# Weight scales in four groups, a weight decode with one join, and weight tiles asked for later

## The chip, the cores and the metric

The kernel runs on one core of one Trainium2 chip. The metric is the device time of one execution in microseconds (us). The engines are named as in the profile: PE (TensorE, matrix products; PEld its weight loads), DVE (VectorE), ACT (ScalarE), POOL (GpSimd) and SP (SyncE, which here only issues DMA transfers). Each takes its own instructions in order.

## The reference

Inputs are q, k, v of shape (4, 8, 768, 64): 4 batches, 8 heads, 768 positions, 64 numbers per head. Each position of q and k is assigned to the nearest of its head's 16 centroids, attention is allowed only within a cluster, and the result goes through a two-layer network with a squared ReLU, 512 to 2048 to 512 numbers per token. The two weight matrices arrive as 64-bit floats.

```python
q_assign = argmax(einsum('bhsd,hcd->bhsc', q_n, c_n), axis=-1)     # q_n, c_n: normalised
k_assign = argmax(einsum('bhsd,hcd->bhsc', k_n, c_n), axis=-1)
mask = q_assign[:, :, :, None] == k_assign[:, :, None, :]
scores = where(mask, matmul(q, k^T) / sqrt(64), -1e9)
attn = softmax(scores, axis=-1)
x = matmul(attn, v)                      # 3072 tokens x 512
h = x @ w_in                             # w_in 512 x 2048
out = (s * max(h, 0)**2 + b) @ w_out     # w_out 2048 x 512
```

## The kernel before, in words

**Units.** Attention is cut into 192 units, each one tile of 128 query rows of one head: the outer loop goes over batch b, chunk c (256 rows), head pair hp, row tile t and head h. A chunk (b, c) has 16 units. A unit is a score `sc` on PE (`scores`, L464: the masked products of Q with all 768 keys, in two fp16 halves), the row maximum on DVE (`maxima`, L473), the exponential on ACT (`exps`, L483, tile `p`), the fp16 high half of `p` (`high`, on POOL, DVE or ACT, L121 or L119, tile `ph`), the low half by subtraction on POOL (`low`, L506), a DMA transpose into `PT` (L508), and the product with V on PE (`values`, L525 to L527, for two units at once, tile `px`), which DVE scales into `xs` (L533 to L537). The first eight units keep fp32 and transpose on PE instead (L503, L520). After four units `finish_x` makes a transposed tile `x`.

**MLP.** The 512 to 2048 to 512 network is worked off in 192 steps, 16 (one per slice ft of 128 hidden numbers) for each of the 12 chunks. A step is 12 products into `h` (`mlp_in`, L583), three activations on ACT (`mlp_relu`), a subtraction on POOL (`mlp_gl`, L598) and 6 products into the accumulator `acc` (`mlp_out`, L610). Step m stands beside unit m + 21 (`LAG`). `acc` has one place in PSUM; at the end of a chunk DVE evicts it into `o` (L618), scaled, and with the bias row added.

**Weights.** For each ft there is a tile of w_in (`wi`) and one of w_out (`wo`), 32 tiles in all. `weights` is a generator that treats one tile per call in a pipeline of three stages: `fetch` (a 512 KB DMA into `wst`), then two calls later `rebase` (ACT takes the high word to a float of another exponent, L203) and `narrow` (DVE shifts it left by 3, L207, then ORs in the low word shifted right by 29, L208), then `bound` one call later. `bound` writes absolute values with ACT (L215, L217; for w_out with a sum along the row), and for w_in takes column sums of them on PE (L220) and their maximum on DVE (L221). When all 32 tiles are through, `finish_w_in` and `finish_w_out` make one power-of-two scale for each matrix. Only then can `wsplit` cut a tile into two fp16 halves (ACT L265, DVE L267), from step 17 on. The main loop calls the generator twice per unit from unit 0 on. The halves take places of the tag `w`, of which there are 33: 32 for the tiles and one more.

**Order.** The program is written unit by unit with generators for the preparation of K, Q and V (`prep_k`, `prep_q`, `prep_v`, started at the steps in `START`); a list scheduler with priorities then fixes one order per engine before the run. The first 20 units have a higher priority (`first_of_all`). Weight loads are issued by SP behind the last transpose.

## Time and profile before

| | us |
|---|---|
| median of 3 runs | 953.16 |
| lowest, highest | 952.39, 954.72 |
| the profiled execution, its own time | 953.86 |
| its span, first to last instruction | 952.2 |
| exponential of unit 0 starts at | 36.37 |
| of unit 20 | 153.36 |
| of unit 32 | 212.11 |
| of unit 60 | 335.75 |

| engine | busy us | share of the span |
|---|---|---|
| PE | 828.6 | 87% |
| ACT | 711.0 | 75% |
| DVE | 626.1 | 66% |
| POOL | 573.0 | 60% |

A line of a group reads: line, engine, operation, output <- inputs, sizes, count | busy us in all, mean ns of one | idle us of the engine just before them, and what ended it. A line of stretches gives start:end, its length, and for each engine its busy us and number of instructions, then the mean granted clock of PE (1.00 is full), the busy share of the DMA engines and GB/s.

### The profile page before, as it was taken

Reading aid. Unit: us, or ns where it says so; the run is one execution under the profiler, and the core shown is the slowest. Engines: PE = TensorE matmul, PEld = TensorE weight load, DVE = VectorE, ACT = ScalarE, POOL = GpSimd, SP = SyncE. Lnnn points to the kernel's source line nnn. Section 1 sums busy time; section 2 is a strip of 40 time slices with the busy share of each in tenths; the row PEclk is TensorE's granted clock in tenths of the full one; section 3 lists DMA queues with packets and bytes.
Section 4 is the critical chain, followed back from the end, with each engine's and each line's share of the span. In section 5 each row is a group of like instructions: output and inputs, shape, how many; then the busy total and the mean of one; then the engine's idle time right before and its main releaser. Section 6 shows DMA issues by size and latency. Waiting matters only on the chain. (4 is left out here: it accounts for less than half of the span.)

```text
span 952.2 us, 22467 instructions
## 1 busy us (share of the span) xinstructions
PE 828.6 (87%) x8625; PEld 579.4 (61%) x8625; DVE 626.1 (66%) x1400; ACT 711.0 (75%) x1390; POOL 573.0 (60%) x596
## 2 busy tenths in 40 slices
PE   0668446988999989999899999999999999999997
PEld 0457324555666667766566666766666766767764
DVE  7797988999677657767865757668666466463100
ACT  4477656887688778987787877978787888789443
POOL 3012545677578566866767758667776765676321
PEclk9965556999999999999999999999999999999999
DMA  6888974876887796968689969758877757777100
GB/s 182 227 215 234 235 179 92 197 151 114 174 167 154 170 201 122 186 147 181 139 165 177 184 142 181 149 130 189 156 153 170 145 116 152 138 165 133 33 23 22
DMA packets 450300, 147.36 MB, mean 155 GB/s; under 512 B 417937, under 2 KB 446609, under 8 KB 450193
## 3 DMA queue, kind: packets, MB, share of 16 engines
q1 hardware_dynamic: 450192, 145.93, 72.2%
q8 instruction: 67, 1.10, 0.5%
q14 instruction: 41, 0.33, 0.1%
HBM read 35.69 MB, written 6.29 MB: 44 GB/s over the span
## 5 line engine op out<-in xcount | busy, mean ns | idle before, releaser
L506 POOL TENSOR_TENSOR ph<-p,ph 128x768 f16<-128x768 f32 x184 | 312.2, 1697 | 123.7 <-ACT ph L119 76.2
L583 PE MATMUL h<-x,wis 128*128 128x256 f16 x2304 | 287.6, 274 | 9.6 <-ACT r L590 8.0
L610 PE MATMUL acc<-wos,g 128*128 128x512 f16 x1152 | 292.6, 379 | 3.2 <-POOL g L598 2.8
L583 PEld LDWEIGHTS <-wis 128*128 128x128 f16 x2304 | 222.2, 98 | 59.5 <-issue 11.3
L598 POOL TENSOR_TENSOR g<-r,g 128x256 f16<-128x256 f32 x192 | 136.6, 713 | 101.7 <-ACT r L593 97.1
L473 DVE TENSOR_REDUCE ssm<-sc 128x1 f32<-128x768 f32 x192 | 181.5, 951 | 24.4 <-PE sc L464 23.6
L483 ACT ACTIVATE p<-sc,ssm,qsm 128x768 f32<-128x768 f32 x192 | 187.7, 978 | 3.4 <-DMA PT<-ph 1.0
L610 PEld LDWEIGHTS <-g 128*128 128x128 f16 x1152 | 103.6, 97 | 87.8 <-POOL g L598 5.7
L480 ACT ACTIVATE ssm<-ssm,lift,qsm 128x1 f32<-128x1 f32 x192 | 73.1, 381 | 92.5 <-DVE ssm L473 91.7
L119 ACT ACTIVATE ph<-p 128x768 f16<-128x768 f32 x164 | 136.1, 830 | 5.8 <-DMA PT<-ph 4.3
L590 ACT ACTIVATE r<-h,cf 128x256 f32<-128x256 f32 x192 | 89.1, 464 | 56.9 <-PE h L583 49.6
L525 PE MATMUL px<-vh,PT 128*128 128x65 f16 x1104 | 120.4, 197 | 12.9 <-DVE xs L537 6.8
L464 PE MATMUL sc<-KA,QA 128*128 128x384 f16 x384 | 99.9, 343 | 26.4 <-ACT p L483 23.4
L526 PE MATMUL px<-vl,PT 128*128 128x64 f16 x1104 | 120.3, 194 | 0.0
L527 PE MATMUL px<-vh,PT 128*128 128x65 f16 x1104 | 120.0, 195 | 0.0
L525 PEld LDWEIGHTS <-PT 128*128 128x128 f16 x1104 | 103.6, 98 | 23.1 <-issue 14.4
L526 PEld LDWEIGHTS <-PT 128*128 128x128 f16 x1104 | 103.3, 100 | 13.2 <-issue 5.1
L464 PE MATMUL sc<-KB,QB 128*128 128x384 f16 x384 | 100.1, 345 | 7.0 <-DMA QB<-qb 7.0
L527 PEld LDWEIGHTS <-PT 128*128 128x128 f16 x1104 | 103.5, 98 | 2.7
L592 ACT ACTIVATE g<-r 128x256 f16<-128x256 f32 x192 | 79.3, 413 | 4.0
L593 ACT ACTIVATE r<-r 128x256 f32<-128x256 f32 x192 | 78.8, 411 | 3.3
L464 PEld LDWEIGHTS <-QA 128*128 128x128 f16 x384 | 35.9, 101 | 54.9 <-issue 29.2
(156 smaller groups left out, 1032.3 us busy)
## 6 DMA issues: line engine op xcount, KB each, us to landing
wst<-in_moe_w_in_dram SPq DMA_DIRECT2D x16, 512.0 KB, 4.5
wst<-in_moe_w_out_dram SPq DMA_DIRECT2D x16, 512.0 KB, 4.5
kn<-in_k_dram SPq DMA_DIRECT2D x16, 384.0 KB, 4.1
qn<-in_q_dram SPq DMA_DIRECT2D x24, 256.0 KB, 3.5
vn<-in_v_dram SPq DMA_DIRECT2D x16, 384.0 KB, 4.1
out_dram<-o SPq DMA_DIRECT2D x12, 512.0 KB, 3.8
PT<-ph SPq DMA_TRANSPOSE x184, 3.5
x<-xn SPq DMA_TRANSPOSE x48, 2.5
```

Of the source, the lines that this page charges most:

```text
L119: A.activation(dst, src, AF.Copy)
L464: last_score[0] = nc.tensor.matmul(sc[:, e, :HALF], X[:, col, :], y[:, h * S + e * HALF : h * S + (e + 1) * HALF], start=st, stop=not st)
L473: last_max[0] = V.tensor_reduce(SM[i // 4][:, 0, j : j + 1], U[i]["sc"], axis=AX.XY, op=ALU.max, negate=True)
L483: last_exp[0] = A.activation(p.rearrange("p (a b) -> p a b", a=2), u["sc"], AF.Exp, bias=bi, scale=u["scale"], **total)
L506: G.tensor_tensor(u["ph"][:, 1, :], u["p"], u["ph"][:, 0, :], op=ALU.subtract)
L525: nc.tensor.matmul(o1, PT[:, kt, :], vh[:, h, kt, : D + 1], start=(kt == 0), stop=False)
L526: nc.tensor.matmul(o, PT[:, kt, :], vl[:, h, kt, :], start=False, stop=False)
L527: nc.tensor.matmul(o1, PT[:, T + kt, :], vh[:, h, kt, : D + 1], start=False, stop=(kt == T - 1))
L583: nc.tensor.matmul(ph[:, :CW], WSP[ft][0][:, wl, kt, :], XS[(b, c, kt)][:, :, xl, :], start=(i == 0), stop=(i == len(terms) - 1))
L590: A.activation(r, ph[:, :CW], AF.Relu, scale=MS[(b, c)][0])
L598: G.tensor_tensor(g[:, 1, :], r, g[:, 0, :], op=ALU.subtract)
L610: nc.tensor.matmul(acc[:, t, :], g[:, gl, rows], WSP[ft][1][:, wl, :], start=(ft == 0 and gl + wl == 0), stop=(ft == NF - 1 and gl == 1))
```

## The change

- **Groups.** The 16 slices ft are split into four groups of four. Each group gets its own scales as soon as its eight tiles are bounded (`finish_group`), so `wsplit(ft)` waits for its own group only. For the first chunk (b + c = 0) `mlp_start` runs once per group, and `mlp_out` accumulates each group apart: `acc` is evicted four times and added up in `o`. Later chunks use one scale for all (`uni`), with a factor per group inside the ReLU.
- **Bounds by PE.** `bound` now works on four tiles at once: PE multiplies the high 16 bits of a tile (read as bf16 with a stride of two) with itself, 16 products into one PSUM bank, and DVE takes one maximum of 512 columns into four. The Abs passes on ACT are gone.
- **One join.** ACT turns the low word into the integer of its three upper bits; DVE joins both words with one shift-and-OR.
- **Places.** The tag `w` has 35 places, three beyond the tiles. `ident` and `ones16` take places of other tags.
- **Asking for tiles.** The main loop calls the generator not at all in units 0 to 3, once in units 4 to 19, then twice.
- **Column sums** of w_out go group by group: four banks' worth of 8 products, each evicted by DVE.
- **High halves** of units 19 to 30 go to POOL (before: DVE for odd, ACT for even units). The starts of batch 1's K and V move from steps 22, 23, 25, 28 to 24, 28, 26, 34.

```diff
     def weight_tile(name):
-        return cp.tile([P, KT, P], F32, tag="w", name=name, bufs=2 * NF + 1)
...
+        return cp.tile([P, KT, P], F32, tag="w", name=name, bufs=2 * NF + 3)
+    GROUP = 4
+    NG = NF // GROUP
...
         A.activation(d["w"], hw, AF.Prelu, scale=2.0 ** -112, alpha=-(2.0 ** 32))
+        A.activation(d["st"][:, :, :, 0], d["st"][:, :, :, 0].bitcast(U32), AF.Copy, scale=0.9375 * 2.0 ** -29, bias=-0.03125)
...
-        V.tensor_scalar(c, c, 3, None, op0=ALU.logical_shift_left)
-        V.scalar_tensor_tensor(c.bitcast(U32), d["st"][:, :, :, 0].bitcast(U32), 29, c.bitcast(U32),
-                               op0=ALU.logical_shift_right, op1=ALU.bitwise_or)
+        V.scalar_tensor_tensor(c.bitcast(U32), c.bitcast(U32), 3, d["st"][:, :, :, 0].bitcast(U32),
+                               op0=ALU.logical_shift_left, op1=ALU.bitwise_or)
...
+    def bound(pairs):
+        pw = ps_h.tile([P, 512], F32, tag="h", name=f"pw_{pairs[0][0]['ft']}")
+        for j, d in enumerate(sum(pairs, [])):
+            wa = d["w"].bitcast(BF16).rearrange("p a (f z) -> p a f z", z=2)[:, :, :, 1]
             for t in range(KT):
...
+                nc.tensor.matmul(pw[:, j * P : (j + 1) * P], wa[:, t, :], wa[:, t, :], start=(t == 0), stop=(t == KT - 1))
+        ft = pairs[0][0]["ft"]
+        V.tensor_reduce(wsq[:, ft : ft + 2, :], pw.rearrange("p (f e q) -> p f e q", e=2, q=P), axis=AX.X, op=ALU.max)
+        if (ft + 2) % GROUP == 0:
+            finish_group(ft // GROUP)
...
+    def finish_group(k):
+        g = [gl[:, e, k : k + 1] for e in range(10)]
+        lc = columns(2, f"w{k}")
+        V.tensor_reduce(lc, wsq[:, k * GROUP : (k + 1) * GROUP, :].rearrange("p f e -> p e f"), axis=AX.X, op=ALU.max)
+        allmax(gsq, lc, f"w{k}")
+        V.tensor_scalar(g[0], gsq[:, 0:1], DM * 1.04, None, op0=ALU.mult)
+        V.tensor_scalar(g[4], gsq[:, 1:2], 1.04, None, op0=ALU.mult)
...
     def wsplit(ft):
-        while narrowed[0] < 2 * NF:
-            next(wgen)
+        k = ft // GROUP
+        while narrowed[0] < 2 * GROUP * (k + 1):
+            next(wgen, None)
...
-    START = {b: [48 * b + x for x in ((-26, -25, -23, -20) if b == 1 else (-40, -38, -32, -28))] for b in range(1, B)}
+    START = {b: [48 * b + x for x in ((-24, -20, -22, -14) if b == 1 else (-40, -38, -32, -28))] for b in range(1, B)}
...
-        copy(G if i < LAG - 2 else V if i < LAG + NF and i % 2 else A, u["ph"][:, 0, :], u["p"])
+        copy(G if i < LAG + 10 else V if i < LAG + NF and i % 2 else A, u["ph"][:, 0, :], u["p"])
...
+        if first:
+            if ft == NF - 1:
                 column_sums()
             for t in range(CT):
+                if k == 0:
+                    V.tensor_scalar(o[:, t, :], acc[:, t, :], e, None, op0=ALU.mult)
+                else:
+                    V.scalar_tensor_tensor(o[:, t, :], acc[:, t, :], e, o[:, t, :], op0=ALU.mult, op1=ALU.add)
...
-        some(wgen, 2)
+        some(wgen, 0 if i < 4 else 1 if i < 20 else 2)
```

How the order moves, at three places. DVE ahead of the maximum of unit 11 (tile `sc_11` before, the second `sc` row in the change; the large numbers only tell tiles apart). Before:

```order
L537 TENSOR_TENSOR xs_1_940<-px_4_925,ssm_4_643 128x128
L207 TENSOR_SCALAR wo8_848<-wo8_848 128x512
L221 TENSOR_REDUCE w1_128<-pw_7_839 128x1
L208 SCALAR_TENSOR_TENSOR wo8_848<-wst_17_849,wo8_848 128x512
L207 TENSOR_SCALAR wi9_856<-wi9_856 128x512
L208 SCALAR_TENSOR_TENSOR wi9_856<-wst_18_857,wi9_856 128x512
L207 TENSOR_SCALAR wo9_900<-wo9_900 128x512
L208 SCALAR_TENSOR_TENSOR wo9_900<-wst_19_901,wo9_900 128x512
L207 TENSOR_SCALAR wi10_908<-wi10_908 128x512
L473 TENSOR_REDUCE ssm_8_864<-sc_11_1021 128x1
```

In the change, from the maximum of unit 10 to that of unit 12:

```order
L493 TENSOR_REDUCE ssm_8_727<-sc_10_806 128x1
L121 COPY PT_7_732<-turned_131 128x384
L557 TENSOR_TENSOR xs_1_787<-px_4_772,ssm_4_552 128x128
L493 TENSOR_REDUCE ssm_8_727<-sc_11_836 128x1
L557 TENSOR_TENSOR xs_1_787<-px_6_850,ssm_4_552 128x128
L493 TENSOR_REDUCE ssm_12_930<-sc_12_923 128x1
```

No weight tile stands between these units any more. Between the maxima of units 0 and 20, DVE had 29 tiles to narrow and now has 13 to join; it had 16 instructions for the two scales and has 24 for the first group's.

DVE between the maxima of units 27 and 29. Before:

```order
L473 TENSOR_REDUCE ssm_24_1825<-sc_27_2024 128x1
L101 TENSOR_REDUCE vm_1_1803<-vn_1_2_1960 128x1
L267 SCALAR_TENSOR_TENSOR wos8_2020<-wo8_848,glob_130,wos8_2020 128x512
L473 TENSOR_REDUCE ssm_28_2131<-sc_28_2118 128x1
L98 TENSOR_REDUCE ksm_1_0_1957<-am_k1_0_2013 128x1
L101 TENSOR_REDUCE vm_1_1803<-vn_1_3_2016 128x1
L68 TENSOR_SCALAR ksm_1_0_1957<-ksm_1_0_1957 128x1
L267 SCALAR_TENSOR_TENSOR wis9_2022<-wi9_856,glob_130,wis9_2022 128x512
L473 TENSOR_REDUCE ssm_28_2131<-sc_29_2195 128x1
```

In the change, a piece behind the maximum of unit 27 (L211 is the join, L282 the split, L221 the bound, L653 the first eviction of `acc`):

```order
L211 SCALAR_TENSOR_TENSOR wi14_1847<-wi14_1847,wst_28_1848 128x512
L282 SCALAR_TENSOR_TENSOR wos8_2036<-wo8_1275,gl_126,wos8_2036 128x512
L602 SCALAR_TENSOR_TENSOR es_0_0_1468<-xm_0_694,gl_126 128x1
L74 TENSOR_SCALAR qsm_0_2_0_1713<-qsm_0_2_0_1713 128x2
L557 TENSOR_TENSOR xs_5_1935<-px_20_1896,ssm_20_1400 128x128
L221 TENSOR_REDUCE wsq_124<-pw_12_1959 128x4
L282 SCALAR_TENSOR_TENSOR wis9_2038<-wi9_1390,gl_126,wis9_2038 128x512
L653 TENSOR_SCALAR o_0_0_1994<-acc_0_0_0_1637,es_0_0_1468 128x512 x2
L389 TENSOR_TENSOR qsm_0_2_0_1713<-qsm_0_2_0_1713,ksm_0_0_147 128x2
L211 SCALAR_TENSOR_TENSOR wo14_1956<-wo14_1956,wst_29_1957 128x512
```

Joins, splits, bounds and evictions now stand together here. Between the maxima of units 20 and 32 DVE had 109 instructions and has 212, 16 joins, 27 splits (before: 24) and 54 + 12 one-column scale instructions among them. In PE's order, 12 steps' `h` and 10.3 steps' `acc` stand ahead of the score of unit 32, before 11 and 9.

SP, from the transpose of unit 9 to that of unit 10. Before, and then in the change:

```order
L508 DMA_TRANSPOSE PT_9_987<-ph_9_980 128x12x128
L85 DMA wst_23_1011<-in_moe_w_out_dram 128x1024
L386 DMA_TRANSPOSE QA_0_1_0_996<-qa_0_1_0_949 128x8x128
L85 DMA wst_24_1019<-in_moe_w_in_dram 128x4x256
L554 DMA_TRANSPOSE x_1_1120<-xn_1_1053 128x4x128
L508 DMA_TRANSPOSE PT_10_1033<-ph_10_1026 128x12x128
```

```order
L528 DMA_TRANSPOSE PT_9_818<-ph_9_811 128x12x128
L89 DMA wst_9_834<-in_moe_w_out_dram 128x1024
L574 DMA_TRANSPOSE x_1_965<-xn_1_868 128x4x128
L406 DMA_TRANSPOSE QA_0_1_0_827<-qa_0_1_0_796 128x8x128
L528 DMA_TRANSPOSE PT_10_848<-ph_10_841 128x12x128
```

Tile 23 and 24 of the weights were asked for here, now it is tile 9.

More of the change, by code (lines that the diff above doesn't have):

```diff
@@ L602, in mlp_out @@
         n = f"{b}_{c}"
-        if ft == 0:
-            MS[(b, c)][2] = ps_a.tile([P, CT, DM], F32, tag="acc", name=f"acc_{n}")
+        first = b + c == 0
+        span = GROUP if first else NF
+        k = ft // GROUP
+        if ft % span == 0:
+            MS[(b, c)][2] = ps_a.tile([P, CT, DM], F32, tag="acc", name=f"acc_{n}_{ft}")
         acc = MS[(b, c)][2]
@@ L608, in mlp_out @@
             rows = slice(t * P, t * P + P)
-            for gl, wl in ((0, 0), (0, 1), (1, 0)):
-                nc.tensor.matmul(acc[:, t, :], g[:, gl, rows], WSP[ft][1][:, wl, :],
-                                 start=(ft == 0 and gl + wl == 0), stop=(ft == NF - 1 and gl == 1))
-        if ft == NF - 1:
-            _, e, acc = MS.pop((b, c))
-            o = sb.tile([P, CT, DM], F32, tag="stage", name=f"o_{n}", bufs=3)
-            if b + c == 0:
+            for gi, wl in ((0, 0), (0, 1), (1, 0)):
+                nc.tensor.matmul(acc[:, t, :], g[:, gi, rows], WSP[ft][1][:, wl, :],
+                                 start=(ft % span == 0 and gi + wl == 0), stop=(ft % span == span - 1 and gi == 1))
+        if ft % span < span - 1:
+            return
+        e = MS[(b, c)][1][:, k : k + 1] if first else MS[(b, c)][1][:, 0:1]
+        if k == 0 or not first:
+            MS[(b, c)].append(sb.tile([P, CT, DM], F32, tag="stage", name=f"o_{n}", bufs=3))
+        o = MS[(b, c)][3]
+        if first:
+            if ft == NF - 1:
                 column_sums()
             for t in range(CT):
+                if k == 0:
+                    V.tensor_scalar(o[:, t, :], acc[:, t, :], e, None, op0=ALU.mult)
+                else:
+                    V.scalar_tensor_tensor(o[:, t, :], acc[:, t, :], e, o[:, t, :], op0=ALU.mult, op1=ALU.add)
+                if ft == NF - 1:
+                    V.tensor_tensor(o[:, t, :], o[:, t, :], bias[0], op=ALU.add)
+        else:
+            for t in range(CT):
                 V.scalar_tensor_tensor(o[:, t, :], acc[:, t, :], e, bias[0], op0=ALU.mult, op1=ALU.add)
+        if ft == NF - 1:
+            MS.pop((b, c))
             nc.sync.dma_start(out[b * S : (b + 1) * S].rearrange("(p t) e -> p t e", t=T)[:, c * CT : (c + 1) * CT, :], o)
```

120 lines of the change are left out of this document (63 added, 57 removed).

## The prediction

> **What bounds the kernel now.** I read the page first, then the busy time of each engine in four stretches of the span, then the groups of instructions in the first two of them, and the timeline of one gap. Page, parts 1 and 2 (busy time; each digit a fortieth of the span):
>
> ```profile
> span 952.2 us, 22467 instructions
> ...
> PE 828.6 (87%) x8625; PEld 579.4 (61%) x8625; DVE 626.1 (66%) x1400; ACT 711.0 (75%) x1390; POOL 573.0 (60%) x596
> ...
> PE   0668446988999989999899999999999999999997
> ...
> DVE  7797988999677657767865757668666466463100
> ...
> PEclk9965556999999999999999999999999999999999
> ```
>
> PE is near full from the seventh or eighth slice on, and before that DVE is the full one, with PE at half its clock. So the places to cut by are the units. The exponentials of L483, one per unit, count 20, 12 and 28 in the first three of these stretches (this is how I chose them: units 0 to 19, 20 to 31, 32 to 59, the rest). I call them A, B, C and D.
>
> ```profile
> L483 ACT ACTIVATE p<-sc,ssm,qsm 128x768 f32<-128x768 f32 x20 | 19.6, 979 | 0.2
> ...
> L483 ACT ACTIVATE p<-sc,ssm,qsm 128x768 f32<-128x768 f32 x12 | 11.7, 975 | 0.0
> ...
> L483 ACT ACTIVATE p<-sc,ssm,qsm 128x768 f32<-128x768 f32 x28 | 27.3, 976 | 0.2
> ```
>
> ```profile
> core 0: us, PE busy (x) PEld busy (x) DVE busy (x) ACT busy (x) POOL busy (x), PEclk, DMA share, GB/s
> 36.30:153.30 117.00, 73.16 (x543) 54.00 (x544) 99.11 (x208) 77.80 (x153) 39.66 (x36) 0.63 0.83 211
> 153.30:212.10 58.80, 51.18 (x523) 34.93 (x523) 54.17 (x101) 46.91 (x92) 39.59 (x35) 0.91 0.78 160
> 212.10:335.70 123.60, 113.62 (x1244) 77.67 (x1243) 90.40 (x197) 96.53 (x184) 85.00 (x84) 1.00 0.75 156
> 335.70:952.20 616.50, 583.21 (x6236) 408.63 (x6234) 353.40 (x805) 476.03 (x939) 398.84 (x401) 1.00 0.70 142
> ```
>
> A costs 5.9 us a unit without any MLP work; C and D cost 4.1 to 4.4 with it. A is DVE's (85% busy) and B is DVE's and PE's together (92% and 87%). C and D are PE's (92%, 95%). What fills DVE in A are the weights, and they also stop it:
>
> ```profile
> L208 DVE SCALAR_TENSOR_TENSOR wi<-wst,wi 128x512 uint32<-128x512 uint32 x14 | 14.7, 1048 | 0.1
> L208 DVE SCALAR_TENSOR_TENSOR wo<-wst,wo 128x512 uint32<-128x512 uint32 x15 | 12.7, 850 | 0.1
> L207 DVE TENSOR_SCALAR wi<-wi 128x512 int32<-128x512 int32 x14 | 9.6, 689 | 3.7 <-ACT wi L203 3.7
> L207 DVE TENSOR_SCALAR wo<-wo 128x512 int32<-128x512 int32 x15 | 6.9, 457 | 4.0 <-ACT wo L203 4.0
> ...
> L221 DVE TENSOR_REDUCE w<-pw 128x1 f32<-128x128 f32 x15 | 4.2, 281 | 1.4 <-PE pw L220 1.4
> ```
>
> The timeline shows what that does to a unit. DVE takes its instructions in order; between the maxima at 79.65 and 95.43 it worked off weight tiles, each when ACT had rebased it (start, duration):
>
> ```profile
> 84.35 0.43 DVE L207 TENSOR_SCALAR wi<-wi 128x512 int32<-128x512 int32 x1 [1.15 <-ACT wi L203]
> ...
> 87.36 0.43 DVE L207 TENSOR_SCALAR wo<-wo 128x512 int32<-128x512 int32 x1 [1.19 <-ACT wo L203]
> ...
> 95.09 0.43 DVE L207 TENSOR_SCALAR wi<-wi 128x512 int32<-128x512 int32 x1 [1.59 <-ACT wi L203]
> 95.43 0.95 DVE L473 TENSOR_REDUCE ssm<-sc 128x1 f32<-128x768 f32 x1
> ```
>
> **The change, part by part.** D keeps its order of instructions nearly word for word, so its 616.5 us stay. The 36 us ahead of A lose three L207 and three Abs, about 1 us that I leave in the range. All else is a sum over A, B and C, against this execution's own span.
>
> *Stage A, DVE.* In the order of the change 13 tiles are joined in A instead of 29, with one DVE instruction each instead of two. L207 goes: 9.6 + 6.9 = 16.5 us. L208 falls from 27.4 to 6 x 1.05 + 7 x 0.85 = 12.3, so 15.1 less. The 15 maxima of L221 go: 4.2. Against this stand four maxima over 512 columns (nearest row 0.686 us), 2.7 us; one group's scales in place of the two old ones, 24 instructions for 16, 1.5 more; and one weight split and two Q splits that come in from B at about 0.95 each, with two short maxima, 3.1.
>
> ```profile
> L101 DVE TENSOR_REDUCE amb_q<-qn 128x2 bf16<-128x512 f32 x24 | 16.4, 685 | 59.6 <-DMA qn<-in_q_dram 59.6
> L98 DVE TENSOR_REDUCE qsm<-am_q 128x2 f32<-128x256 f32 x24 | 10.0, 418 | 8.8 <-PE am_q L97 8.8
> ```
>
> Net 28.5 less: 99.1 becomes 70.6. DVE's idle time was 17.9 us, 9.1 of it ahead of L207 and L221. Of that I keep 13/29 of 7.7, 3.5, so 12.3 idle and a stretch of 83. Waits that the weights had covered (the next unit's maximum on its score, 2.3 us now) will show, so I take 85. The ends: 75, if nearly all idle goes, and 100, if only half of the DVE time comes off the path. **Gain of A: 32 (17 to 42).** ACT does not stand in the way: it loses 29 Abs and gains 13 integer passes, nearest the rebase rows, and its waits for weight DMAs shrink with the tiles:
>
> ```profile
> L203 ACT ACTIVATE wo<-wst 128x512 f32<-128x512 f32 x15 | 9.9, 661 | 7.0 <-DMA wst<-in_moe_w_out_dram 7.0
> L215 ACT ACTIVATE wab<-wo 128x512 bf16<-128x512 f32 x15 | 9.4, 625 | 2.6 <-DVE wo L208 2.5
> ```
>
> The price of the integer pass is not in the trace: 0.63 (Abs) to 0.98 (the exponential, 768 columns), taken as 0.66, and 13 of them against 29 Abs leave ACT shorter at either end. PE gets 16 products per four tiles where it had 8. In A that is 13 tiles' worth, some 52 for 60 at L220, and PE idles 44 us there; nothing. Without that cover they would cost what the 60 do now, if a product of two strided halves takes no longer, and 16 us if each takes the 0.3 that its row shows:
>
> ```profile
> L220 PE MATMUL pw<-wab,ones 128*128 128x128 bf16 x60 | 9.0, 297 | 9.8 <-ACT wab L217 7.9 <-DVE w L221 1.8
> ```
>
> *Stage B, DVE.* Here the work comes back. The order puts 16 joins between the maxima of units 20 and 32, where there was none. At 0.945, the mean of L208, they cost 15.1 (0.85 to 1.21 each, the latter from the split row below). Three more splits: 3.3. Four wide maxima: 2.7. Three reductions over 256 columns: 1.3. Three groups' scales and three more starts of the first chunk: 87 instructions on one column, 0.15 busy each but partly overlapped, 5 to 13, taken as 9. Four evictions of the accumulator, 0.745 each: 3.0. Off go six casts (3.8), and the loads of batch 1 that start later: two maxima of K, two of V, a one-hot and two Q splits, less one maximum, 6.4.
>
> ```profile
> L267 DVE SCALAR_TENSOR_TENSOR wis<-wi,glob,wis 128x512 f16<-128x512 f32 x10 | 12.1, 1210 | 0.7 <-ACT wis L265 0.7
> ...
> L267 DVE SCALAR_TENSOR_TENSOR wos<-wo,glob,wos 128x512 f16<-128x512 f32 x10 | 9.8, 982 | 0.6 <-ACT wos L265 0.5
> L121 DVE CAST ph<-p 128x768 f16<-128x768 f32 x6 | 3.8, 630 | 0.0
> ...
> L618 DVE SCALAR_TENSOR_TENSOR o<-acc,xm,bias 128x512 f32<-128x512 f32 x24 | 17.0, 745 | 46.6 <-PE acc L610 46.2
> ...
> L60 DVE TENSOR_SCALAR xm<-xm 128x1 f32<-128x1 f32 x12 | 1.8, 151 | 0.3
> ```
>
> That is 24.2 more: 54.2 becomes 78.4, and at the stage's present 92% busy 85 us. The ends: 77 (short instructions overlapped, all idle gone) and 98 (joins at the split's price, and DVE stopped at each group by its own reductions through PE). **Loss of B: 26 (18 to 39).** Queued behind DVE are each unit's maximum, so ACT's exponential, and the accumulator's evictions, behind which PE cannot start the next group. The three places for halves let ACT run ahead of DVE's half, for which it waits 9.8 us there now, and are worth nothing while DVE is full:
>
> ```profile
> L265 ACT ACTIVATE wis<-wi,glob 128x512 f16<-128x512 f32 x11 | 7.9, 717 | 4.6 <-DVE wos L267 4.5
> L265 ACT ACTIVATE wos<-wo,glob 128x512 f16<-128x512 f32 x10 | 7.2, 718 | 5.3 <-DVE wis L267 5.3
> ```
>  The high halves of units 19 to 30 that move to POOL cost it 12 x 1.024 = 12.3 us: 39.6 becomes 52 of 85, so POOL is no bound by its own sum.
>
> ```profile
> L121 POOL CAST ph<-p 128x768 f16<-128x768 f32 x11 | 11.3, 1024 | 18.6 <-ACT p L483 16.6 <-issue 2.0
> ```
>
> *Stage C.* PE bounds it. At the score of unit 32 the new order stands one input step, 1.3 output steps and one pair of values further; a step's half is 1.31 us:
>
> ```profile
> 816.79 1.31 PE h L583 x12
> ...
> 844.70 1.31 PE acc L610 x6
> ```
>
> So some 4 us less PE work are left. The column sums now pass through one bank four times instead of once, three more evictions of about 0.75, and their cover is the MLP that the order puts between them: 0 to 2.2, taken as 1. Further on, chunk 2 waits for its inputs whatever PE has done ahead. **C: 3 less (8 less to 8 more).**
>
> Sum: 952.2 - 32 + 26 - 3 = 943.2 us span. The profiled execution took 953.86, 1.7 more than its span, and the median is 953.16, so the forecast is **944 us**; the ends of the likeliest case, with A and B each moved half-way, are 936 and 950.
>
> **The rivals.** *DVE shut out by POOL in B (slower).* The same split takes 836 ns (wis, four of them) in A and 1210 in B, where POOL is busy 67% of the time instead of 34%; so the two engines already get in each other's way. The change puts 12.3 us of casts on POOL in just this stage, against 43 DVE instructions of that kind. If DVE stands for all of it, and each unit's maximum behind it, B is 85 + 12.3 = 97 and with the stops at the groups 101: 960 us. It decides from B above 96, where A's gain and C's 3 are used up. Against it: POOL would still be free for a third of the stage.
>
> ```profile
> L267 DVE SCALAR_TENSOR_TENSOR wis<-wi,glob,wis 128x512 f16<-128x512 f32 x4 | 3.3, 836 | 0.0
> ```
>
> [...]
>
> *PE's clock falls again in B (no change).* In A the granted clock was 0.63 with PE 63% busy, in B 0.91 with 87%. PE's 51.2 us in B grow by 64 products, 9.6 by L220's row, to 61 of 85, 72%, between the two. At half the clock the 12 steps take 12 x 2 x 1.31 = 31 us more, PE needs 92, B is about 95 and the kernel ends at 954. Against it: idle times of PE in B would be many and short, and once up, the clock stayed up from the eighth slice to the end. [...]
>
> *A falls to DVE's sum (much faster).* If weights were all that separated the units, A is 75 and B, whose DVE then meets its own waits in parallel, 79: 952.2 - 42 + 20 - 3 = 927, about 928. The 14.8 us that PE waited in A for exponentials speak against so dense a stage:
>
> ```profile
> L464 PE MATMUL sc<-KA,QA 128*128 128x384 f16 x40 | 14.4, 456 | 14.9 <-ACT p L483 14.8
> ```
>
> **Chances.** The forecast (936 to 950) 0.47; much faster 0.18; no change, by the clock or by A and B cancelling, 0.15; slower by POOL 0.15, by anything else 0.05. A measurement of this kernel can tell 0.3%, 2.9 us, from no change. So faster 0.65, same 0.15, slower 0.20. The range takes in the much faster case and the slower rival: 928 to 960.
>
> **What would show it.** In the changed profile L207's kind of row is gone; the twentieth exponential stands 25 to 40 us earlier; the next twelve units take 77 to 98 us with DVE above 90% busy; the joins there take 0.85 to 1.2 us; PEclk shows nines from the fourth or fifth slice on. The sum is wrong if A does not shorten by 17 us, if B passes 98, or if D differs from 616 by more than 3.

## The result, and the profile after

| | before | after |
|---|---|---|
| median of 4 runs, us | 953.94 | 1005.69 |
| lowest, highest | 952.39, 957.18 | 1001.97, 1007.24 |
| span of the profiled execution | 952.2 | 1003.2 |

The changed kernel is slower: 1.0532 times the time before, 95% interval 1.0491 to 1.0573. Forecast were 944 us in a range of 928 to 960. Parts 1 and 2 of its page (busy time; fortieths of the span):

```profile
span 1003.2 us, 22641 instructions
...
PE 851.3 (85%) x8696; PEld 590.7 (59%) x8696; DVE 611.3 (61%) x1468; ACT 707.5 (71%) x1368; POOL 574.8 (57%) x607
...
PE   0576557687899699989988989999889899999997
...
DVE  6685597888556855756766657757755556464100
...
PEclk9976658799899799999999999999999999999999
```

DVE shows a single 9 in the first ten slices where before there were five, so it is relieved there; but PE shows its first 9 only in the twelfth slice (before: the eighth). And PE's clock has dents up to the fourteenth slice, where before it had none after the seventh. The four stretches of the prediction, cut at the exponentials of units 0, 20, 32 and 60:

```profile
core 0: us, PE busy (x) PEld busy (x) DVE busy (x) ACT busy (x) POOL busy (x), PEclk, DMA share, GB/s
38.20:141.10 102.90, 68.05 (x549) 51.11 (x550) 69.89 (x169) 58.47 (x109) 38.88 (x37) 0.71 0.76 170
141.10:234.30 93.20, 70.54 (x630) 47.10 (x630) 77.64 (x208) 66.26 (x130) 47.83 (x48) 0.84 0.75 169
234.30:373.40 139.10, 115.52 (x1204) 77.95 (x1203) 92.39 (x201) 92.23 (x172) 81.62 (x81) 0.91 0.79 146
373.40:1003.20 629.80, 590.36 (x6236) 410.69 (x6234) 346.25 (x805) 477.23 (x939) 397.61 (x401) 0.99 0.77 139
```

| us | ahead of A | A | B | C | D | span |
|---|---|---|---|---|---|---|
| before | 36.3 | 117.0 | 58.8 | 123.6 | 616.5 | 952.2 |
| forecast | 36.3 | 85 | 85 | 120.6 | 616.5 | 943.2 |
| after | 38.2 | 102.9 | 93.2 | 139.1 | 629.8 | 1003.2 |

DVE's busy time came out as forecast, 69.9 for 70.6 in A and 77.6 for 78.4 in B. The lengths did not: every stretch is longer than its term, D too, whose order of instructions hardly changed.

*A.* The timeline shows in what form the time stands there, here between two exponentials at 91.68 and 98.44 (start, duration; in brackets the idle time before and what ended it):

```profile
89.29 0.96 DVE L493 TENSOR_REDUCE ssm<-sc 128x1 f32<-128x768 f32 x1 [0.52 <-PE sc L484]
...
91.33 2.62 DVE L190 SCALAR_TENSOR_TENSOR qa<-qn,qsm,qb 128x256 f16<-128x256 f32 x2
...
94.00 1.18 DVE L211 SCALAR_TENSOR_TENSOR wi<-wi,wst 128x512 uint32<-128x512 uint32 x1
...
95.23 0.61 PE L219 MATMUL pw<-wi 128*128 128x128 bf16 x4 [5.87 <-DVE gl L61]
...
95.64 0.52 PE L484 MATMUL sc<-KA,QA 128*128 128x384 f16 x1
...
98.15 0.39 ACT L500 ACTIVATE ssm<-ssm,lift,qsm 128x1 f32<-128x1 f32 x1 [4.40 <-DVE ssm L493]
```

PE, in order, stands 5.87 us before the bound's products of a tile (L219); the join that makes the tile (L211) stands on DVE behind two splits and a group's scales; and the next unit's score (L484), that of unit 13, stands behind the products. ACT's order puts the scale of unit 13 (L500, at 98.15) ahead of the exponential of unit 12, whose own scale was done at 90.7; so this exponential too waits for the products. I had written that those products cost nothing because PE idles anyway, and had not named what queues behind them. DVE's idle time in A, 33 us, stands mostly where it waits for PE, and for 4.8 us only ahead of the joins; the two largest rows:

```profile
L493 DVE TENSOR_REDUCE ssm<-sc 128x1 f32<-128x768 f32 x21 | 20.0, 953 | 8.7 <-PE sc L484 8.5
...
L121 DVE COPY PT<-turned 128x384 f32<-128x384 f32 x8 | 4.4, 553 | 6.6 <-PE turned L523 6.4 <-issue 0.2
```

*B.* The exponentials of units 25 and 26 stand 20.1 us apart (3.4 before). ACT's timeline there:

```profile
171.70 0.37 ACT L500 ACTIVATE ssm<-ssm,lift,qsm 128x1 f32<-128x1 f32 x1
...
172.33 0.97 ACT L503 ACTIVATE p<-sc,ssm,qsm 128x768 f32<-128x768 f32 x1
...
179.88 0.37 ACT L500 ACTIVATE ssm<-ssm,lift,qsm 128x1 f32<-128x1 f32 x1
...
183.64 0.67 ACT L206 ACTIVATE wo<-wst 128x512 f32<-128x512 f32 x1 [1.05 <-DMA wst<-in_moe_w_out_dram]
...
188.66 0.67 ACT L206 ACTIVATE wi<-wst 128x512 f32<-128x512 f32 x1 [3.80 <-DMA wst<-in_moe_w_in_dram]
...
192.43 0.98 ACT L503 ACTIVATE p<-sc,ssm,qsm 128x768 f32<-128x768 f32 x1
```

The scale at 171.70 is that of unit 26, the one at 179.88 already that of unit 27. So the exponential of unit 26 could have run at 172.1, and all of the 20.1 us are ACT's fixed order: before it stand five rebases, each with its integer pass, six first halves of splits, six passes of the first chunk, the scale of unit 27 and two halves of Q. Two of the rebases wait for a weight tile that is still on its way, 4.9 us together; most of the rest is work. DVE, with the counterparts, has its own row of work between the maxima of units 27 and 28 (16.2 us apart):

```profile
L282 DVE SCALAR_TENSOR_TENSOR wis<-wi,gl,wis 128x512 f16<-128x512 f32 x3 | 2.9, 952 | 0.0
L282 DVE SCALAR_TENSOR_TENSOR wos<-wo,gl,wos 128x512 f16<-128x512 f32 x3 | 2.2, 741 | 0.0
...
L653 DVE TENSOR_SCALAR o<-acc,es 128x512 f32<-128x512 f32 x2 | 1.4, 732 | 0.0
L211 DVE SCALAR_TENSOR_TENSOR wi<-wi,wst 128x512 uint32<-128x512 uint32 x2 | 1.4, 679 | 0.3 <-ACT wst L207 0.3
L211 DVE SCALAR_TENSOR_TENSOR wo<-wo,wst 128x512 uint32<-128x512 uint32 x2 | 1.4, 676 | 0.0
```

*C.* It has the mirror image. Between the exponentials of units 40 and 41, 22.4 us apart (7.7 before), only PE works all the time, at full clock, on MLP steps and column sums. The scale of unit 41 is done at 276.0, but ACT's order puts the activations of these steps, which wait for PE's `h` one by one, ahead of its exponential:

```profile
275.62 0.39 ACT L500 ACTIVATE ssm<-ssm,lift,qsm 128x1 f32<-128x1 f32 x1 [1.76 <-DVE ssm L493]
...
294.56 0.97 ACT L503 ACTIVATE p<-sc,ssm,qsm 128x768 f32<-128x768 f32 x1
```

```profile
272.10:294.60 22.50, 22.50 (x177) 14.52 (x176) 10.81 (x25) 12.54 (x27) 7.48 (x10) 1.00 0.26 61
```

And where PE had stood, its clock was low, 0.50 for the next 6.7 us where it was 0.99 before: the first product after an idle time of 4.83 us, and the stretches before and after it:

```profile
249.81 0.20 PE L415 MATMUL pq<-cT,QA 128*128 128x16 f16 x1 [4.83 <-DMA QA<-qa]
```

```profile
244.90:249.80 4.90, 0.07 (x3) 0.00 (x0) 4.37 (x14) 3.37 (x6) 2.06 (x2) 0.99 0.88 134
249.80:256.50 6.70, 5.40 (x61) 3.53 (x61) 5.24 (x14) 2.99 (x4) 4.72 (x6) 0.50 0.73 137
```

At 178.0 us, without one long idle time, the clock was at half as well, after a stretch in which PE's longest idle time was 0.9 us and it was busy for 1.58 us of 3.4:

```profile
174.60:178.00 3.40, 1.58 (x16) 0.95 (x16) 3.40 (x22) 1.89 (x5) 0.81 (x2) 1.00 0.78 259
178.00:181.40 3.40, 3.40 (x40) 2.36 (x39) 3.40 (x9) 3.40 (x9) 1.35 (x2) 0.50 1.18 301
```

### The profile page after: what moved, and what is told of

Its sections match the earlier page's. It is cut to its first block, busy times and chain, and to the rows that moved or that the text cites. A ratio compares the mean times of both kernels' runs of the same rounds, so it can differ in the third digit from the quotient of the medians.

```text
span 1003.2 us, 22641 instructions
## 1 busy us (share of the span) xinstructions
PE 851.3 (85%) x8696; PEld 590.7 (59%) x8696; DVE 611.3 (61%) x1468; ACT 707.5 (71%) x1368; POOL 574.8 (57%) x607
## 2 busy tenths in 40 slices
DMA packets 450300, 147.37 MB, mean 147 GB/s; under 512 B 417936, under 2 KB 446608, under 8 KB 450192
## 3 DMA queue, kind: packets, MB, share of 16 engines
q1 hardware_dynamic: 450192, 145.93, 76.0%
## 5 line engine op out<-in xcount | busy, mean ns | idle before, releaser
L526 POOL TENSOR_TENSOR ph<-p,ph 128x768 f16<-128x768 f32 x184 | 311.6, 1694 | 118.7 <-ACT ph L119 85.5
L610 PE MATMUL h<-x,wis 128*128 128x256 f16 x2304 | 293.1, 277 | 14.7 <-ACT r L617 9.4
L640 PE MATMUL acc<-wos,g 128*128 128x512 f16 x1152 | 297.9, 383 | 5.4 <-ACT g L619 3.0
L610 PEld LDWEIGHTS <-wis 128*128 128x128 f16 x2304 | 225.5, 99 | 68.0 <-issue 18.7
L625 POOL TENSOR_TENSOR g<-r,g 128x256 f16<-128x256 f32 x192 | 132.9, 694 | 136.0 <-ACT r L620 126.6
L500 ACT ACTIVATE ssm<-ssm,lift,qsm 128x1 f32<-128x1 f32 x192 | 73.2, 381 | 134.5 <-DVE ssm L493 134.0
L545 PE MATMUL px<-vh,PT 128*128 128x65 f16 x1104 | 125.0, 199 | 13.7 <-DVE xs L557 7.5
L119 ACT ACTIVATE ph<-p 128x768 f16<-128x768 f32 x158 | 131.2, 830 | 6.0 <-DMA PT<-ph 5.4
L546 PE MATMUL px<-vl,PT 128*128 128x64 f16 x1104 | 125.0, 197 | 0.0
L547 PE MATMUL px<-vh,PT 128*128 128x65 f16 x1104 | 124.5, 198 | 0.0
L545 PEld LDWEIGHTS <-PT 128*128 128x128 f16 x1104 | 106.5, 100 | 23.9 <-issue 15.3
L484 PE MATMUL sc<-KA,QA 128*128 128x384 f16 x384 | 101.8, 349 | 21.2 <-ACT p L503 18.0
L546 PEld LDWEIGHTS <-PT 128*128 128x128 f16 x1104 | 106.3, 102 | 15.2 <-issue 7.0
L547 PEld LDWEIGHTS <-PT 128*128 128x128 f16 x1104 | 106.4, 100 | 2.6 <-issue 0.3
L484 PE MATMUL sc<-KB,QB 128*128 128x384 f16 x384 | 102.3, 351 | 4.0 <-DMA QB<-qb 4.0
L484 PEld LDWEIGHTS <-QA 128*128 128x128 f16 x384 | 35.8, 102 | 47.1 <-issue 23.2
```

What stands on the lines that cost most here:

```text
L119: A.activation(dst, src, AF.Copy)
L484: last_score[0] = nc.tensor.matmul(sc[:, e, :HALF], X[:, col, :], y[:, h * S + e * HALF : h * S + (e + 1) * HALF], start=st, stop=not st)
L526: G.tensor_tensor(u["ph"][:, 1, :], u["p"], u["ph"][:, 0, :], op=ALU.subtract)
L545: nc.tensor.matmul(o1, PT[:, kt, :], vh[:, h, kt, : D + 1], start=(kt == 0), stop=False)
L546: nc.tensor.matmul(o, PT[:, kt, :], vl[:, h, kt, :], start=False, stop=False)
L547: nc.tensor.matmul(o1, PT[:, T + kt, :], vh[:, h, kt, : D + 1], start=False, stop=(kt == T - 1))
```

## The experiments

All stretches below are in us, cut as above; D runs to the end. Where no interval is given, a row is one profiled execution. Two things limit what single rows can tell. The four timed runs of the changed kernel lie 5.3 us apart. And A varies more than that: p33_al and al_pc below have the same order of instructions on PE up to about unit 20, and A took 97.9 in one and 108.4 in the other. Differences in A under 10 us between such kernels carry nothing.

| run | ahead | A | B | C | D | span |
|---|---|---|---|---|---|---|
| before_again | 37.1 | 116.6 | 58.3 | 125.5 | 616.4 | 954.0 |
| pace2 | 36.6 | 129.4 | 75.1 | 138.1 | 629.7 | 1009.0 |
| group16 | 37.1 | 117.6 | 76.3 | 129.6 | 629.2 | 989.7 |
| noprod | 38.1 | 104.0 | 82.8 | 140.9 | 626.7 | 992.6 |
| places33 | 36.5 | 100.5 | 94.6 | 142.4 | 623.4 | 997.4 |
| poolcast | 38.2 | 99.6 | 84.5 | 139.6 | 624.5 | 986.4 |
| g16_pcst | 36.6 | 118.2 | 64.9 | 130.2 | 622.4 | 972.3 |
| b_join | 35.7 | 120.6 | 56.1 | 129.2 | 617.2 | 958.7 |
| b_shift64 | 36.9 | 117.6 | 59.7 | 129.2 | 629.6 | 973.1 |
| p33_al | 35.8 | 97.9 | 95.8 | 137.4 | 609.4 | 976.2 |
| b_align | 35.1 | 116.6 | 58.6 | 125.7 | 616.0 | 952.1 |
| all_undo | 37.8 | 129.8 | 60.5 | 140.5 | 629.3 | 997.8 |
| b_shift256 | 35.9 | 116.1 | 58.0 | 125.5 | 617.5 | 953.0 |
| al_pc | 37.0 | 108.4 | 87.8 | 138.8 | 614.0 | 986.0 |
| al_g8 | 36.5 | 107.2 | 77.6 | 135.8 | 613.6 | 970.8 |
| al_g16 | 36.1 | 117.6 | 57.2 | 131.6 | 612.5 | 955.0 |
| late20 | 35.6 | 93.3 | 119.4 | 147.9 | 612.5 | 1008.8 |
| b_pebound | 36.8 | 118.7 | 57.9 | 132.4 | 611.7 | 957.5 |

### First: pace, groups, products

before_again is the kernel before, unchanged.

> The kernel before, profiled once more on the chip that runs the next three, to compare its last stretch (unit 60 on, 616.5 us in the first profile, 629.8 in the changed kernel though the order of instructions is the same there). If the transposes are slower by the state of the chip, this run too shows some 630 us behind unit 60 and about 957 in all. If the changed kernel itself makes them slower (other places in SBUF), this run shows 616 and 953.

pace2:

```diff
-        some(wgen, 0 if i < 4 else 1 if i < 20 else 2)
+        some(wgen, 2)
```

> The changed kernel with the generator called twice per unit from unit 0 again, all else kept. Theory 'pace': asking later moved 16 joins from units in which PE has nothing else to do to units in which it has the MLP; then units 20 to 31 go from 93 to about 70 us, units 0 to 19 stay near 103 to 110, and the kernel takes 975 to 985. Theory 'products': the waits of PE's own bound products cost the time wherever they stand; then units 0 to 19 become longer, to 115 or more, and the sum stays within 10 us of 1005.

group16 has the same line, and

```diff
-    GROUP = 4
+    GROUP = NF
```

> The changed kernel with one group of 16 slices and the old pace of two tiles per unit: one scale, one accumulation per chunk, splits only when all 32 tiles are bounded. The join, the bounds by PE, the three places, the POOL casts and the later starts stay. Theory 'groups': the four groups' scales, evictions and their order cost the loss of units 20 to 59; then this kernel is at 950 to 965. Theory 'products': it stays above 980, since the bound products are all there.

noprod leaves the true bound of the weights out: the 16 products of four tiles multiply a constant, so they wait for no join.

```diff
-            wa = d["w"].bitcast(BF16).rearrange("p a (f z) -> p a f z", z=2)[:, :, :, 1]
+            wa = identb
...
-                nc.tensor.matmul(pw[:, j * P : (j + 1) * P], wa[:, t, :], wa[:, t, :], start=(t == 0), stop=(t == KT - 1))
+                nc.tensor.matmul(pw[:, j * P : (j + 1) * P], wa, wa, start=(t == 0), stop=(t == KT - 1))
```

> The changed kernel, but the bound products take the identity matrix instead of the weight tile, so that they are as many and as long and wait for no join; what is left out is the true bound of the weights, the scales become a constant. Theory 'products' (PE stands in order at a product whose tile is not joined yet, 20 us in units 0 to 19, with the next score behind it): units 0 to 19 go from 103 to 85 to 90 us and the kernel to 975 to 990. Theory 'pace': units 20 to 31 keep their 93 us and the kernel gains less than 10.

Times: 955.67, 1010.75, 991.42 and 994.28 us, beside 956.56 of the kernel before. The pace is no cause of the loss: without it A + B is 204.5 instead of 196.1, A longer by 26.5 and B shorter by 18.1. One group is 19 us faster than four at the old pace (group16 and pace2), but far from the 950 to 965 of its theory. The products' wait on PE costs about 10 us, all of it in B by these single rows; A stays at 104.0 without it, so the wait at 95.23 above is where A's time shows, and not what makes it. The second surprise is D: 627 to 630 in all three variants, 616.4 in the kernel before run beside them. So it is not the chip, and none of the three edits.

### Second: places, casts, the join

What all variants shared were the places in SBUF and the casts on POOL. places33 and poolcast:

```diff
-        return cp.tile([P, KT, P], F32, tag="w", name=name, bufs=2 * NF + 3)
+        return cp.tile([P, KT, P], F32, tag="w", name=name, bufs=2 * NF + 1)
```

> The changed kernel with 33 places for weight tiles and halves as before, in place of 35; all else stays. Theory 'layout' (the two further places move the attention's tiles in SBUF, and the transposes from ph to PT take longer there): from unit 60 to 191 about 542 us again instead of 555.7, transposes landing in 3.4 us at the median instead of 3.96, the whole about 990. Rival 'something else of the change' (the identity and the ones in places of other tags, no tiles for absolute values): 555 us there again and 3.9 to 4.0, the whole 1000 to 1010. If the places help the splits, units 20 to 31 take some us longer than 93.

```diff
-        copy(G if i < LAG + 10 else V if i < LAG + NF and i % 2 else A, u["ph"][:, 0, :], u["p"])
+        copy(G if i < LAG - 2 else V if i < LAG + NF and i % 2 else A, u["ph"][:, 0, :], u["p"])
```

> The changed kernel with the high halves of units 19 to 30 back on DVE and ACT. Theory 'POOL shuts DVE out' (the rival of the prediction): units 20 to 31 fall from 93 to 80 or less, although DVE gets 3.8 us of work back. Rival 'what the order puts between two maxima': 93 to 97, the whole 1002 to 1010.

g16_pcst is group16 with this edit, and the old starts:

```diff
-(-24, -20, -22, -14) if b == 1
+(-26, -25, -23, -20) if b == 1
```

> One group of 16, two tiles asked for per unit, the high halves of units 19 to 30 on DVE and ACT and the starts of batch 1 at the old steps: of the change are left the join, the bounds by products on PE, the places and the column sums' form. Before this, with the casts on POOL and the late starts, units 20 to 31 took 76.3 us against 58.8 of the kernel before. Theory 'casts and starts': 59 to 63, the whole about 976. Rival 'join and bounds': 72 to 77, the whole 986 to 992. Units 0 to 19 about 117 in either case; from unit 60 on 555.

b_join is the kernel before with the changed kernel's rebase and narrow, the decode with one join.

> The kernel before with the one-join decode alone: 29 of the 32 shifts of DVE in the first 20 units go, 16.5 us by their rows, and ACT gets an integer pass per tile, 0.66 us or so, 19 us in that stretch. Theory 'DVE bounds the first stage': units 0 to 19 take 100 to 105 instead of 117, the whole 938 to 943. Rival 'ACT and the weights' arrival bound it as well': 112 to 117, the whole 949 to 955. From unit 60 on 542 us in either case, unless the join itself is what slows that stretch.

Times: 999.21, 988.15, 974.0 and 961.62, beside 957.45. With 33 places the transposes from ph to PT still land late (median 3.87 us in D), so it isn't the number of places. Without the casts on POOL the kernel is 17 us faster, with four groups (1004.93 to 988.15) as with one (991.42 to 974.0, starts included); 8.6 and 11.4 of it are in B. B's 84.5 in poolcast lies between its two expectations. That is near the size of the rival that I had put at 0.15, but its mechanism, DVE shut out for the casts' 12.3 us, doesn't show. The split rows of B, of poolcast

```profile
L282 DVE SCALAR_TENSOR_TENSOR wis<-wi,gl,wis 128x512 f16<-128x512 f32 x12 | 14.4, 1199 | 0.0
```

and of the changed kernel, with all casts on POOL:

```profile
L282 DVE SCALAR_TENSOR_TENSOR wis<-wi,gl,wis 128x512 f16<-128x512 f32 x12 | 11.8, 984 | 0.0
```

With more work on POOL the split is quicker in this pair, not slower. A single split does get longer beside POOL: in the B of the changed kernel, the 15 splits during which POOL had no instruction took 0.73 to 0.75 us each, the 10 others 0.72 to 1.99, 1.21 on average. But over all kinds of DVE instruction, at equal numbers of each, those of B cost 1.4 us less in this pair with the casts on POOL, not 12.3 more. What the casts may do instead is queue. POOL's groups in B of the changed kernel:

```profile
L121 POOL CAST ph<-p 128x768 f16<-128x768 f32 x11 | 10.2, 925 | 0.5 <-ACT p L503 0.5
L625 POOL TENSOR_TENSOR g<-r,g 128x256 f16<-128x256 f32 x14 | 9.9, 707 | 28.9 <-ACT r L620 28.9
```

POOL stands 28.9 us before `g`, waiting for ACT's `r` (15.6 in poolcast), and casts that ACT or DVE would have made stand behind it in order. That this wait is the cause is argued from these rows, not shown.

The join alone does not help: DVE is rid of 11.9 us in A and ACT gets 13.7, and A is 120.6 instead of 117.0, longer than either expectation. So taking work off DVE did not shorten A; but this work went to ACT, and the run can't tell DVE's work from the sum of both.

### Third: where the tiles lie in SBUF

The built programs place the tag `big` (p, ph, PT and the sources qa, qb, ka of the other transposes, 11 places of 3072 bytes) at byte 107008 of each partition before, which is 209 x 512, and at 114336 in the change, 160 past a multiple of 512: constants and tiles ahead of it came and went. In group16 and g16_pcst it is 64 past, in places33 160 past. The first three runs below move tiles and change nothing else: a pad moves all tiles behind it, and the order on every engine is the same. b_shift64:

```diff
+    const([P, 16], F32, "pad")
     rev = const([P, C], F32, "rev")
```

> The kernel before with 64 bytes put ahead of all its tiles in SBUF, nothing else: same instructions, same order on every engine. The tiles of the tag big (p, ph, PT, QA's and KA's sources) then begin at 64 bytes past a multiple of 512, as in the run with one group, instead of at a multiple of 512. Theory 'place in SBUF': the transposes from ph to PT land in 3.8 to 4.0 us at the median instead of 3.43, units 60 to 191 take 547 to 551 us instead of 542.4, the whole is 5 to 14 us slower, 960 to 968. Rival 'the program': nothing changes, 953 to 957.

p33_al is places33 with `const([P, 88], F32, "pad")` there, 352 bytes.

> The changed kernel with 33 places and 352 bytes put ahead of all tiles, so that the tiles of the tag big begin at a multiple of 512 as in the kernel before; order of instructions as with 33 places alone (997.4 us span, 549.4 from unit 60 to 191, transposes 3.87). Theory 'place in SBUF': transposes 3.4 to 3.5 us, 541 to 545 us from unit 60 on, the whole span 985 to 991. Rival: 548 to 551, 995 to 1000.

b_align is the kernel before with unused tiles of 96, 448 and 352 bytes ahead of KA, the staged weights and x.

> The kernel before with gaps of 96, 448 and 352 bytes between tags, so that KA, KB, QA, QB, the staged weights, the outputs and x begin at multiples of 512 too (before: 416, 416, 416, 416, 480, 480 and 128 past one); same instructions and order. Theory 'place in SBUF' for every tile that a transpose writes: QA, QB, KA, KB and x land some 0.3 us earlier, the whole is 2 to 6 us faster than before, 948 to 952. If only the place of ph and PT matters, or the place does not matter: within 2 us of before.

all_undo is the changed kernel with the edits of pace2, poolcast and the old starts together, four groups kept.

> The changed kernel with two tiles asked for per unit from unit 0 on, the high halves of units 19 to 30 on DVE and ACT and the old starts: against the run with one group the four groups alone are added. Theory 'groups cost by what they put between scores and maxima': span 982 to 990, with units 20 to 59 some 10 to 15 us longer than the 195.1 of one group. Rival 'only together with the casts on POOL': 970 to 976, units 20 to 59 within 4 us of 195.

The first result is the clearest of the study: with 64 bytes ahead the kernel before takes 1.0191 times as long (1.0149 to 1.0233; medians 974.84 and 956.39), more than the 960 to 968 that I expected. The page of b_shift64, parts 1, 3 and 6 (share of the DMA engines' time; median from issue to landing):

```profile
span 973.1 us, 22467 instructions
...
q1 hardware_dynamic: 450192, 145.93, 77.2%
...
PT<-ph SPq DMA_TRANSPOSE x184, 4.0
```

and of the kernel before:

```profile
q1 hardware_dynamic: 450192, 145.93, 72.2%
...
PT<-ph SPq DMA_TRANSPOSE x184, 3.5
```

The same 450192 packets and 145.93 MB take 5 points more of the engines' time. The changed kernel shows 76.0% and 4.0 us; p33_al, whose order is that of places33, is back at

```profile
span 976.2 us, 22643 instructions
...
q1 hardware_dynamic: 450192, 145.93, 72.2%
...
PT<-ph SPq DMA_TRANSPOSE x184, 3.4
```

and takes 978.03 us where places33 took 999.21, 19.0 of the difference in C and D. b_align is the kernel before in time, 1.0008 (0.9992 to 1.0024): its KA, KB, QA, QB and x, all transposed into, now begin at multiples of 512 and land about as before (QA 3.0 us in both, x 2.5, KA 3.4; QB 3.6 for 3.5, KB 4.0 for 4.2). So in this run the place of those targets made no difference to the time. That it is the tag big follows by exclusion only: the tags of the loaded K and V and of the weights' places lie as far past a multiple of 512 as big in every run here.

all_undo took 999.69. Against g16_pcst four groups add 25.5 us of span, more than I expected, and not where I expected it: 11.6 in A, 4.4 less in B, 17.2 in C and D, whose tiles lie 160 past in one and 64 past in the other.

### Fourth: at an equal place

b_shift256 has 256 bytes ahead. al_pc is p33_al with poolcast's edit; al_g8 is al_pc with `GROUP = 8`; al_g16 is g16_pcst with 33 places; each has a pad so that the tag big begins at a multiple of 512.

> The kernel before with 256 bytes put ahead of all its tiles, same instructions and order. With 64 bytes the transposes landed in 3.93 us instead of 3.43 and units 60 to 191 took 555.6 us instead of 542.4. Theory 'multiples of 256 are enough': 3.43 and 542 to 543, the whole 953 to 957. Rival 'multiples of 512 are needed': 3.8 or more and 548 to 556, the whole 962 to 975.

> The changed kernel with 33 places, 352 bytes ahead (tiles of the tag big at multiples of 512) and the high halves of units 19 to 30 on DVE and ACT. Without the last edit its span was 976.2, units 20 to 31 took 95.8. If the casts on POOL cost what they did at the other place (18.5 us of span, 8.6 of it in units 20 to 31): span 956 to 962, units 20 to 31 in 85 to 88. If they cost less at the better place, since the halves' transposes are quicker: 965 to 976.

> As the run before it, with two groups of 8 slices in place of four of 4; pad chosen so that the tiles stand at the same places. Theory 'the groups' short instructions, evictions and reductions are what fills DVE in units 20 to 31': that stretch is 5 to 9 us shorter than with four groups, the whole 5 to 10 us faster, about 951. Rival 'the later first group holds up the first chunk': units 20 to 59 longer, the whole 960 to 975.

> 33 places, tiles of the tag big at multiples of 512, one group, two tiles per unit from unit 0 on, casts and starts as before: of the change are left the join, the bounds by products on PE and the column sums' form. At the worse place it took 972.3 us of span (units 0 to 19 118.2, 20 to 31 64.9, 32 to 59 130.2, 60 to 191 548.4). Theory 'the rest of its loss is the place': 950 to 955, 117, 59, 124, 542. Rival 'join and bounds cost by themselves' (the join alone made the kernel before 6 us longer): 958 to 963.

Times: 954.73, 987.78, 972.5 and 956.75, beside 954.83. With 256 bytes nothing is lost:

```profile
span 953.0 us, 22467 instructions
...
q1 hardware_dynamic: 450192, 145.93, 72.2%
...
PT<-ph SPq DMA_TRANSPOSE x184, 3.5
```

So 256 past a multiple of 512 does as well as 0 here (954.73 us beside 954.83), and 64 past does not (974.84 beside 956.39); with 160 past, in places33, the page has 3.9 us from issue to landing, where p33_al, put back, has 3.4. Why the place counts, no run here shows.

al_g16 is 2.8 us of span from before: the join, the bounds by PE and the column sums cost next to nothing. Two groups with the new pace and starts bring it to 970.8, four to 986.0, and B to 77.6 and 87.8; that is in the range of the rival, not the 951 of the theory. What the pace and the starts do at an equal place without the groups was not run. al_pc's whole is no measure of the casts, since A is 10.5 longer than in p33_al; B is 8.0 shorter, as at the other place, but B + C + D only 2.0 (13.4 there). What the casts cost outside B at an equal place stays open. And the split goes the other way here, longer with the casts on POOL (p33_al, then al_pc):

```profile
L283 DVE SCALAR_TENSOR_TENSOR wis<-wi,gl,wis 128x512 f16<-128x512 f32 x12 | 12.1, 1007 | 0.2 <-ACT wis L281 0.2
```

```profile
L283 DVE SCALAR_TENSOR_TENSOR wis<-wi,gl,wis 128x512 f16<-128x512 f32 x11 | 9.1, 825 | 0.0
```

Over all kinds of DVE instruction, at equal numbers, it is 3.0 us more in this pair: a loss of the rival's size on DVE shows in neither.

### Last: what bounds A

late20 is p33_al with no tile asked for before unit 20:

```diff
-        some(wgen, 0 if i < 4 else 1 if i < 20 else 2)
+        some(wgen, 0 if i < 20 else 2)
```

> The changed kernel with 33 places and 352 bytes ahead (units 0 to 19 took 97.9 us there, DVE 69.9 busy and 28 idle), and no weight tile asked for before unit 20 but the three that stand ahead of unit 0: ten joins, four wide maxima and a group's scales leave that stretch, some 14 us of DVE; they come back in units 20 to 31, which take far longer. Theory 'the weights in units 0 to 19 still stop everything, since PE, DVE and ACT stand in order at a tile that arrives late': that stretch falls by their DVE time and by most of the waits at joins and products, to 72 to 80. Rival 'without much DVE work the chain of each unit (score, maximum, scale, exponential) bounds it, at half PE clock': 86 to 95.

b_pebound is al_g16 with the old decode of two DVE instructions.

> As the run with one group at the better place (955.0 us of span), with the old decode (DVE's shift and OR, no integer pass on ACT): of the change are left the bounds by products on PE and the column sums' form. Against the kernel before ACT is rid of 32 passes of 0.63, DVE of 15 short maxima. Theory 'ACT and DVE together bound units 0 to 19, the join only moves work between them': that stretch takes 106 to 113 instead of 117, the whole 942 to 950. Rival 'the products' waits on PE take what ACT gains': 115 to 119, the whole 952 to 957.

late20's time is 1010.96. Its A, and what is waited for in it (total, times, longest):

```profile
35.60:128.90 93.30, 57.57 (x441) 42.08 (x441) 51.35 (x108) 41.45 (x78) 37.56 (x37) 0.70 0.54 121
```

```profile
ACT ssm L501 <- DVE ssm L494: 48.9, 17, 8.3
...
DVE ssm L494 <- PE sc L485: 18.8, 12, 5.5
...
PE sc L485 <- ACT p L504: 13.1, 7, 2.7
```

Only three tiles are left in A, DVE is busy 51.4 of 93.3 us, and A is still 93.3 long. The waits are now those of the units themselves: the scale on ACT for the maximum on DVE, the maximum for the score on PE, the score for the exponential, with PE at 0.70 of its clock. One row can't carry much more: 93.3 is within 10 us of p33_al's 97.9, and DVE still has other work in the stretch. But it is above the 85 that I forecast, with hardly any weight work left.

b_pebound is 1.0029 times the kernel before (1.0011 to 1.0048). A takes 118.7, though ACT is busy 59.8 us in it and not 77.8:

```profile
36.80:155.50 118.70, 71.87 (x620) 54.29 (x621) 98.23 (x212) 59.79 (x108) 42.91 (x37) 0.69 0.81 208
```

Four kernels with 29 tiles in A (before 117.0, b_join 120.6, al_g16 117.6, b_pebound 118.7) have DVE busy for 99.1, 87.2, 84.3 and 98.2 and ACT for 77.8, 91.5, 75.6 and 59.8. Neither moves A by itself. b_pebound came out in the range of its rival, though, that PE's products take what ACT gains, and both it and al_g16 have these products; so what does hold A is not shown. It goes with the number of tiles: 29 tiles 117 to 121, 15 or 16 tiles 98 to 108, three tiles 93. (With four groups and 29 tiles, pace2 and all_undo, it is 129 to 130, which was not followed up.) No version that I ran beats the kernel before.

## Why the prediction was wrong

**D, "its 616.5 us stay": wrong by 13.3.** The order stayed, as said, but not the place of its tiles. The same program 64 bytes further takes 629.6 in D; the changed kernel with 33 places, put back, takes 609.4. I never looked at where the tiles come to lie, though the list of changes (constants dropped, places added) names what moves them. Over the whole kernel the place is worth 18 to 21 us at an equal order (18.5 between the medians of the kernel before, 20.9 between its profiled spans, 21.2 from places33 to p33_al).

**A, gain 32: it was 14, at the better place 19 (p33_al) or 9 (al_pc).** "99.1 becomes 70.6" came out (69.9), in part by luck: 15 joins of 0.77 us stood in the stretch, not 13 of 0.945. The step that failed is the idle time, "12.3 idle and a stretch of 83": DVE idled 33.0 us, 8.5 of it for scores and 6.4 for PE's transposes. For waits that the weights had covered the prediction had allowed 2 us, from 83 to 85. The lower end was off as well: half of 28.5 us is a stretch of 103, not 100, and 102.9 is what came. I took DVE's share of 85% for a bound. In b_join and al_g16 DVE had 12 and 15 us less to do and A was no shorter. late20 still needs 93 with three tiles in the stretch, so the rival of A at 75 falls too.

**B, loss 26: it was 34.4.** The sum, 78.4, came out again (77.6), with terms off both ways: 14 joins for 16, six evictions for four, splits of 0.93 us for 1.10. Without the casts on POOL B takes 84.5 and 87.8, near the 85 forecast. So the edit that I costed at nothing, the casts, holds the miss of 8, by a mechanism that stays open. And I looked at DVE alone, with each exponential behind its maximum. In the changed kernel's B an exponential stood on ACT for 9.1 us on average after its own scale was done (before 3.5, in poolcast 6.0, p33_al 9.4, al_pc 5.6): it waited for its place in ACT's order, as in the 20.1 us above, and not for DVE's maximum. I had a rival of that size with a reason that the runs don't bear out: with the casts on POOL the split was shorter in one pair and longer in the other.

**C, 3 less: it was 15.5 more.** "Some 4 us less PE work are left" counted the order at unit 32 alone; PE's busy time in C is 115.5 for 113.6, and the catch-up stands in front of the exponential of unit 41, which is 22.4 us behind that of unit 40. The clock adds to it: at 0.91 over 139.1 us, up to 12.5 us of full speed are missing, where before it was 1.00. Part of C's loss comes back later: at the better place C + D is 746.8 against 740.1 before.

**The clock as a rival, 954:** its mechanism came true in part (0.84 in B against 0.91, 0.91 in C), on top of the loss and not in place of it. My argument against it, that PE's idle times in B would be many and short, did not hold at 178.0 us, where the clock was at half and none of the idle times before it was over 0.9 us. **The short rows** were right: the joins in B took 0.88 and 0.90 us, and rows like L207's on DVE are gone.

Of the 51.0 us between the spans, then, about 21 are the place of the tiles in SBUF, as measured with 33 places; with 35 the better place was not run. The rest is the split into groups with the pace and starts that go with it, not told apart from each other: at an equal place one group with the old pace stands at 955.0, two groups at 970.8, four at 976.2 to 986.0. The casts' 8 us of B are in the changed kernel's share; how they and A's variation add up in the whole isn't settled. What inside the groups costs the time, ACT's order in B or the wider first chunk, is argued above from single gaps and not shown by a run of its own.

## What to carry to other kernels

After any edit that adds or drops a constant or a tile, look where the sources of the DMA transposes come to lie, and pad them back to a place at which a run lost nothing (here 0 and 256 bytes past a multiple of 512) before comparing times: here 64 bytes were worth 1.9%, more than most edits. An engine at 85% is not a bound until taking work off it shortens the stretch; the cheapest test is a kernel with that work moved out altogether, which shows what is left. And in an order fixed beforehand a busy sum can be right to 1% and the stretch wrong by 20%, since what counts is who stands behind each late instruction. Follow an exponential back from its start: if its inputs were long ready, it waited for its place on its own engine.
